# Attention and MoE on one core: weight conversion moved to the start, out of two PSUM banks, and the first batch in two halves

## Chip, cores and metric

The kernel runs on one NeuronCore of a Trainium2 chip. The metric is the time of one execution on the device, in microseconds. Five engines have queues of their own: PE (TensorE), DVE (VectorE), ACT (ScalarE), POOL (GpSimd) and SP, which here only starts DMAs.

## What is computed

Top-32 attention over 8 batches of 8 heads, 576 tokens and 64 columns a head, and behind it one MoE layer with a squared ReLU over all 4608 tokens. The weights come in 64-bit floats, everything else in 32-bit.

```python
scores = scale * np.matmul(q, k.transpose(0, 1, 3, 2))
kth = np.partition(scores, -top_k, axis=-1)[..., -top_k:-top_k + 1]
scores = np.where(scores >= kth, scores, -1000000000.0)
attn = np.exp(scores - np.max(scores, axis=-1, keepdims=True))
attn = attn / (np.sum(attn, axis=-1, keepdims=True) + 1e-09)
x = np.matmul(attn, v)          # tokens x 512, all heads of a token side by side
r = np.maximum(x @ w_in, 0.0)   # w_in 512 x 2048
out = (s * (r * r) + b) @ w_out # w_out 2048 x 512
```

## The kernel before

**Attention.** Two heads make a pair, four pairs a batch. A pair has nine tiles of 128 query rows (tile 4 mixes the last 64 rows of both heads), so a batch has 36 tiles and the kernel 288. Each tile goes through scores on PE (L363), a copy to SBUF on ACT (L369), the top-32 threshold on DVE (eight L375, then L382 to L391), a check on ACT and POOL (L409, L415), exp on ACT (L423), the mask on DVE (L433), transposes on PE (L462, L463) and the product with V. Where a product has to be exact, each operand is split into a high and a low part; batch 0 ("whole", WHOLE = 1) does without the split of the probabilities. A batch is one piece per pair (FULL), but the last batch is cut in HALVES: the first five tiles of all four pairs, then the last four of each.

**MoE.** Blocks of 256 tokens (18), each of 16 chunks of 128 hidden columns, so 288 chunks. A chunk is 12 matmuls into the one buffer `h` (L604), ReLU and square on ACT (L610, L613), a split on POOL (L617, L621) and 6 matmuls into the two buffers `ops` (L627). A block starts when the attention rows of its 256 tokens have been stored for all four pairs.

**Weights.** `w_in` and `w_out` are 64 pieces of 128 x 256. A piece is loaded (L300) into one of four `x` buffers, made 32-bit by three bit operations on DVE (L306, L309, L312; the intermediate `tmp` lies in SBUF, tag `rt`), checked for far exponents (ACT L319, L323, and a PE matmul L326 that accumulates all 64 pieces in the `h` buffer), and split (ACT L329, POOL L332). The column sums of `w_out` for the bias are PE matmuls (L315) that accumulate in both `ops` buffers. So `h` and `ops`, the MoE's PSUM banks, are taken until the last of the 64 pieces is done.

**Order.** Nothing is in loops on the chip. A planner (`Graph.order`) lays the operations of all engines out by a list schedule: of those that could start next on an engine, within SLACK ns of the first, the one with the lowest key. Keys are tile numbers (a chunk's is TURN0 + chunk / TURNS, a weight piece's WTURN * n / 64) plus an offset by kind from PARTS, where each kind also has the planner's slot and duration in ns. LOCK names kinds of which the planner lets DVE and POOL run only one at a time. Each engine then runs its list strictly in that order.

## Time and profile before

| | |
|---|---|
| time, median of 3 runs | 1673.21 us (1672.47 to 1674.39) |
| the profiled execution | 1674.74 us |
| its span, first to last instruction | 1673.0 us |
| mean granted TensorE clock | 0.960 |
| busy: PE, DVE, ACT, POOL | 1486.4, 1393.2, 1251.0, 1292.3 us |

"Busy" is the union of an engine's instructions in time; matmuls are pipelined, so the mean duration of one is longer than the distance between two. The span falls into stages with different work, so the shares over the whole span say little; the section of rows cuts it into six stretches, and counts in them how many tiles and chunks were done.

### The profile page before, as it was taken

To read this page: it belongs to the slowest core of one execution; us is meant where nothing else is said; L and a number is where in the kernel's file an instruction comes from. 1 tells how busy PE (TensorE), PEld (TensorE's weight loads), DVE (VectorE), ACT (ScalarE), POOL (GpSimd) and SP (SyncE) were. 2 spreads that over 40 slices of the span, in tenths; PEclk is the share of its full clock that TensorE was granted. 3 is DMA by queue.
4 is the path that set the end of the run, shared out by engine and by line. 5 is a ranking of instruction groups with operands and counts; after the bars stand their busy time and mean duration, and the time that the engine had idled before them with its cause. 6 is when DMAs were issued, how large, how long until landed. Compare 5 with 4: busy or idle time off the path is not lost.

```text
span 1673.0 us, 33649 instructions
## 1 busy us (share of the span) xinstructions
PE 1486.4 (89%) x9361; PEld 1285.3 (77%) x9361; DVE 1393.2 (83%) x6055; ACT 1251.0 (75%) x2842; POOL 1292.3 (77%) x2111
## 2 busy tenths in 40 slices
PE   3676776799999998989999999999999999999997
PEld 2444444687888887978888888888888889878886
DVE  5999988899999999989999999998989977797000
ACT  4787877887878887877787888887877877786221
POOL 3666665788889887888888988888878988898432
PEclk9986877799999999999999999999999999999999
DMA  4333323222121222122322222222222233442000
GB/s 134 90 94 117 101 88 100 84 58 76 45 83 50 76 60 70 53 83 59 84 54 77 59 73 59 70 58 77 71 57 68 77 105 90 117 131 72 30 13 15
DMA packets 102115, 124.45 MB, mean 74 GB/s; under 512 B 30240, under 2 KB 65056, under 8 KB 101920
## 3 DMA queue, kind: packets, MB, share of 16 engines
q1 hardware_dynamic: 101920, 122.22, 25.5%
q8 instruction: 77, 1.26, 0.3%
q14 instruction: 118, 0.97, 0.2%
HBM read 60.56 MB, written 21.50 MB: 49 GB/s over the span
## 4 chain that ended last, share of the span: by engine, by line
PE 37%; DVE 33%; ACT 9%; DMA 6%; POOL 5%; issue 5%; SPq 4%; POOLq 0%; ACTq 0%; DVEq 0%
PE h L604 12%; PE ops L627 11%; DVE cand L375 8%; DVE e L433 6%; DVE chk L429 4%; DVE pl L473 4%; PE tp L462 4%; PE s_ps L363 4%; SPq L709 2%; DMA kr<-in_kq_dram 2%; ACT sc L369 2%; ACT sg L409 2%; PE av L493 1%; DVE cand L384 1%; POOL wt L415 1%
## 5 line engine op out<-in xcount | busy, mean ns | idle before, releaser
L415 POOL TENSOR_TENSOR wt<-sc,sg 128x576 f32<-128x576 f32 x288 | 402.6, 1398 | 50.3 <-ACT sg L409 17.5
L604 PE MATMUL h<-x,wih 128*128 128x256 f32 x2176 | 421.6, 288 | 11.4 <-ACT rt L610 8.3
L375 DVE MAX8 cand<-sc 128x8 f32<-128x72 f32 x2304 | 392.2, 219 | 44.5 <-ACT sc L369 43.4
L604 PEld LDWEIGHTS h<-x,wih 128*128 128x128 f32 x2176 | 347.1, 190 | 32.9 <-ACT rt L610 17.5
L604 PE MATMUL h<-x,wil 128*128 128x256 f32 x1088 | 307.6, 283 | 0.0
L433 DVE SCALAR_TENSOR_TENSOR e<-sc,chk,e 128x576 f32<-128x576 f32 x288 | 281.5, 979 | 1.7
L409 ACT ACTIVATE sg<-sc,nb 128x576 bf16<-128x576 int16 x288 | 222.0, 771 | 51.3 <-POOL wt L415 25.4
L462 PE MATMUL tp<-idr,e 128*128 128x128 f32 x1152 | 188.4, 288 | 64.3 <-DVE e L433 35.1
L369 ACT ACTIVATE sc<-s_ps 128x576 f32<-128x576 f32 x288 | 185.7, 645 | 64.5 <-DVE e L433 41.1
L429 DVE MAX8 chk<-wt 128x8 f32<-128x584 f32 x288 | 218.2, 758 | 10.9 <-POOL wt L419 9.7
L423 ACT ACTIVATE e<-sc,nb 128x576 f32<-128x576 f32 x288 | 222.0, 771 | 7.1 <-POOL nb L403 3.8
L621 POOL TENSOR_TENSOR gl<-rt,gh 128x256 fp32r<-128x256 f32 x288 | 217.3, 757 | 12.2 <-PE ops L627 1.3
L462 PEld LDWEIGHTS tp<-idr,e 128*128 128x128 f32 x1152 | 135.0, 146 | 106.0 <-issue 35.0
L604 PEld LDWEIGHTS h<-x,wil 128*128 128x128 f32 x1088 | 207.2, 190 | 0.0
L627 PE MATMUL ops<-woh,gh 128*128 128x512 f32 x576 | 195.2, 406 | 7.2 <-DVE osb L634 4.5
L610 ACT ACTIVATE rt<-h 128x256 f32<-128x256 f32 x288 | 109.1, 379 | 122.7 <-PE h L604 112.9
L473 DVE TENSOR_TENSOR pl<-tp,ph 128x512 fp32r<-128x512 f32 x252 | 172.9, 686 | 30.6 <-ACT ph L468 26.1
L363 PE MATMUL s_ps<-ka,qs 128*128 128x288 f32 x512 | 162.0, 330 | 33.8 <-ACT sc L369 14.8
L627 PE MATMUL ops<-woh,gl 128*128 128x512 f32 x576 | 188.7, 399 | 0.9 <-POOL gl L621 0.8
L627 PE MATMUL ops<-wol,gh 128*128 128x512 f32 x576 | 187.6, 398 | 0.0
L617 POOL TENSOR_SCALAR gh<-rt 128x256 fp32r<-128x256 f32 x288 | 123.2, 430 | 79.1 <-PE ops L627 57.1
L468 ACT ACTIVATE ph<-tp 128x512 fp32r<-128x512 f32 (+1 forms) x288 | 169.5, 589 | 11.7 <-PE tp L462 9.6
(98 smaller groups left out, 3362.9 us busy)
## 6 DMA issues: line engine op xcount, KB each, us to landing
kr<-in_kq_dram SPq DMA_DIRECT2D x72, 288.0 KB, 3.2
ka<-kb SPq DMA_DIRECT2D x72, 144.0 KB, 3.3
kb<-ka SPq DMA_DIRECT2D x72, 144.0 KB, 3.1
out_dram<-osb SPq DMA_DIRECT2D x36, 256.0 KB, 2.0
kr<-in_v_dram SPq DMA_DIRECT2D x56, 160.0 KB, 2.4
x<-in_moe_w_in_dram SPq DMA_DIRECT2D x32, 256.0 KB, 3.1
qs<-ka SPq DMA_DIRECT2D x128, 64.0 KB, 2.0
qs<-kb SPq DMA_DIRECT2D x128, 64.0 KB, 2.0
```

The source lines that it names most:

```text
L363: nc.tensor.matmul(flat[:, cs], st, kx[:, cs], start=(m == 0), stop=(m == last))
L369: nc.scalar.activation(t.sc, t.flat, AF.Identity)
L375: nc.vector.max(t.cand[:, g * 8 : g * 8 + 8], t.sc[:, g * GW : (g + 1) * GW])
L409: nc.scalar.activation(t.sg, t.sc.bitcast(I16)[:, 1::2], AF.Sign, bias=t.half, scale=-1.0, accum_out=t.cnt[:, 0:1])
L415: nc.gpsimd.tensor_tensor(out=t.wt[:, :S], in0=t.sc, in1=t.sg, op=ALU.mult)
L423: nc.scalar.activation(t.e, t.sc, AF.Exp, bias=t.nb, scale=scale)
L429: nc.vector.max(t.pair.chk[:, t.i, 0:PADS], t.wt)
L433: nc.vector.scalar_tensor_tensor(t.e, t.sc, chk[:, PADS - 1 : PADS], t.e, op0=ALU.is_ge, op1=ALU.mult, accum_out=chk[:, PADS : PADS + 1])
L462: nc.tensor.transpose(tp[:, c, :], t.e[:, c * P : (c + 1) * P], idf)
L473: nc.vector.tensor_tensor(out=pl[:, :, dst], in0=t.tp, in1=ph[:, :, dst].bitcast(F32), op=ALU.subtract)
L604: nc.tensor.matmul(k.h, wi[a][:, cc, fs], k.x[cc][:, c, :], start=(cc == 0 and i == 0), stop=(cc == NCC - 1 and i == 2))
L627: nc.tensor.matmul(k.ops[t], g[fc][:, t * P : (t + 1) * P], wo[w][:, fc, :], start=(fc == 0 and i == 0), stop=(fc == NFC - 1 and i == 2),)
```

## The change

Five things are done.

1. Two PSUM banks are no longer used for sums over the weights. The far check (`far1`) squares in place on ACT and lets ACT add up each piece (two halves for a piece of `w_out`) into one of 96 columns of an `osb` buffer; `farmax` reduces these. The column sums are 32 matmuls of 512 columns in one run (`colsum`), with a matrix of ones and the split `w_out`, into the `av` buffer, after the last piece has been split; `b` is multiplied in behind it.
2. The intermediate of the bit operations is an `ops` buffer in PSUM, not an SBUF tile; the second operation writes it again, and the third writes the result to SBUF.
3. The pieces come in another sequence (for each 256 columns of `w_in`, its four pieces, then the four of `w_out` that belong to them), with WTURN 21.3 for 40. Some use the four `x` buffers, the rest three more in the space of `pl`, which the first batch doesn't use; so the first `low` of batch 1 waits for all weight work (`wend`), and the first output matmul of the MoE's block 0 for all bit operations (`wbits`).
4. Batch 0 is cut in HALVES as batch 7 is: its first five tiles of four pairs, then the last four. Batch 0's Q, K and V are loaded twice, and its Q and K split twice.
5. The planner's numbers are new: offsets, durations (those of SP and of the bit operations longer), SLACK for PE and ACT, TURN0 and TURNS, and LOCK without the bit operations.

Of the table of numbers one line stands here.

```diff
-    "wload": ("SP", 100, 3500, -0.43), "bits0": ("DVE", 195, 275, -11.69), "bits1": ("DVE", 330, 412, 6.37), "bits2": ("DVE", 325, 405, -2.64),
+    "wload": ("SP", 460, 3300, -2.22), "bits0": ("DVE", 324, 420, -18.25), "bits1": ("DVE", 330, 425, 4.31), "bits2": ("DVE", 330, 415, -7.95),
...
-LOCK = {"mask", "bits0", "bits1", "bits2", *(x for x, y in PARTS.items() if y[0] == "POOL")}
-SLACK = {"PE": 0, "DVE": 86, "ACT": 0, "POOL": 0, "SP": 0}
-TURN0, TURNS = 49.4, 0.992
-WTURN = 40
+LOCK = {"mask", *(x for x, y in PARTS.items() if y[0] == "POOL")}
+SLACK = {"PE": 40, "DVE": 86, "ACT": 14, "POOL": 0, "SP": 0}
+TURN0, TURNS = 51.4, 1.007
+WTURN = 21.3
 
 LATE = (16,)
-BUFS = dict(ph=1, pl=1, p4=1, avu=2, avl=1, x=4, osb=1, sc=4, wt=1, e=2, kr=1, sg=1, rt=2, gh=2, gl=2, vst=2, ka=2, kb=2, qs=2, s_ps=1, tp=1, tq=1, av=1, h=1, ops=2, cand=2, wl=3, m2=2, cnt=3, nb=2, chk=2, ri=2)
+EARLY = 49
+BUFS = dict(ph=1, pl=1, p4=1, avu=2, avl=1, x=4, wraw=3, osb=1, sc=4, wt=1, e=2, kr=1, sg=1, rt=2, gh=2, gl=2, vst=2, ka=2, kb=2, qs=2, s_ps=1, tp=1, tq=1, av=1, h=1, ops=2, cand=2, wl=3, m2=2, cnt=3, nb=2, chk=2, ri=2)
...
+    ones = const.tile([P, P], F32R, name="ones")
+    nc.scalar.activation(ones, idt, AF.Identity, scale=0.0, bias=1.0)
     bias = const.tile([P, DM], F32, name="bias")
-    brow = [ps_o.tile([P, DM], F32, name="ops", tag="ops", bufs=2) for _ in range(2)]
     mid = const.tile([P, 1], F32, name="mid")
-    wfar = ps_h.tile([P, WCH], F32, name="h", tag="h", bufs=1)
+    nc.gpsimd.memset(mid, -64.0)
...
-    wsteps = [(wi, w_in, cc, f) for cc in range(NCC) for f in range(DFF // WCH)]
-    wsteps += [(wo, w_out, fc, e) for fc in range(NFC) for e in range(DM // WCH)]
+    wsteps = []
+    for f in range(DFF // WCH):
+        wsteps += [(wi, w_in, cc, f) for cc in range(NCC)]
+        wsteps += [(wo, w_out, f * WCH // P + x, e) for x in range(WCH // P) for e in range(DM // WCH)]
+    def early(n):
+        return n < EARLY and n % 7 < 4
...
         def load(w):
-            w.raw = sb.tile([P, 2 * WCH], I32, name="x", tag="x", bufs=BUFS["x"])
+            if w.early:
+                w.raw = sb.tile([P, 2 * WCH], I32, name="x", tag="x", bufs=BUFS["x"])
+            else:
+                c0 = 2 * WCH * (sum(not early(n) for n in range(w.n)) % 3)
+                w.raw = p_buffers(True)[1].rearrange("p a b -> p (a b)").bitcast(I32)[:, c0 : c0 + 2 * WCH]
             w.hw, w.lw = w.raw[:, 1::2], w.raw[:, 0::2]
             nc.sync.dma_start(
                 out=w.raw, in_=w.src.bitcast(I32)[w.a * P : (w.a + 1) * P, 2 * w.c * WCH : 2 * (w.c + 1) * WCH]
             )
 
         def bits0(w):
-            w.tmp = sb.tile([P, WCH], I32, name="rt", tag="rt", bufs=BUFS["rt"])
+            w.tmp = ps_o.tile([P, DM], F32, name="ops", tag="ops", bufs=2).bitcast(I32)[:, :WCH]
             nc.vector.tensor_scalar(w.tmp, w.hw, 5, 2, op0=ALU.logical_shift_left, op1=ALU.logical_shift_right)
 
         def bits1(w):
-            nc.vector.scalar_tensor_tensor(w.lw, w.lw, 29, w.tmp, op0=ALU.logical_shift_right, op1=ALU.bitwise_or)
+            nc.vector.scalar_tensor_tensor(w.tmp, w.lw, 29, w.tmp, op0=ALU.logical_shift_right, op1=ALU.bitwise_or)
 
         def bits2(w):
-            nc.vector.scalar_tensor_tensor(w.lw, w.hw, -(1 << 30), w.lw, op0=ALU.bitwise_and, op1=ALU.bitwise_or)
-        def colsum(w):
-            nc.tensor.matmul(brow[w.c][:, :WCH], bmat, w.lw.bitcast(F32), start=(w.a == 0), stop=(w.a == NFC - 1))
...
         def far1(w):
-            w.ck = sb.tile([P, WCH], F32R, name="gh", tag="gh", bufs=BUFS["gh"])
-            nc.scalar.activation(w.ck, w.hw.bitcast(F32), AF.Square, bias=mid)
-        def far2(w):
-            nc.tensor.matmul(wfar, idr, w.ck, start=(w.n == 0), stop=(w.n == len(wsteps) - 1))
+            if not far:
+                far.append(sb.tile([P, DM], F32, name="osb", tag="osb", bufs=BUFS["osb"]))
+            n = 1 if w.dst is wi else 2
+            for x in range(n):
+                cs = slice(x * WCH // n, (x + 1) * WCH // n)
+                k = (w.a * (DFF // WCH) + w.c) if n == 1 else 32 + (w.a * 2 + w.c) * 2 + x
+                nc.scalar.activation(
+                    w.hw.bitcast(F32)[:, cs], w.hw.bitcast(F32)[:, cs], AF.Square, bias=mid, accum_out=far[0][:, k : k + 1]
+                )
...
+    wcol = [None]
+    def colsum():
+        wcol[0] = ps_a.tile([P, 512], F32, name="av", tag="av", bufs=1)
+        for fc in range(NFC):
+            for x in range(2):
+                nc.tensor.matmul(wcol[0], ones, wo[x][:, fc, :], start=(fc + x == 0), stop=(fc == NFC - 1 and x == 1))
+    def bias_out():
+        nc.scalar.activation(bias, wcol[0], AF.Identity, scale=b_col)
...
-        parts = HALVES if b == B - 1 else (FULL,)
+        parts = HALVES if b in (0, B - 1) else (FULL,)
...
-        if pr.part == 2:
+        if pr.part == 2 and not pr.whole:
...
-    walls, wlast = {}, {}
-    whole_h, whole_o = Buf("h"), [Buf("ops") for _ in range(DM // WCH)]
+    walls, wfar, farb, wbits = {}, [], Buf("osb"), []
     for n in range(len(wsteps)):
         w, key = Weight(n), WTURN * n / len(wsteps)
-        raw, rt, ck = Buf("x"), Buf("rt"), Buf("gh")
-        ld = part("wload", key - 6, w.load, new=[raw])
+        raw, rt = Buf("x" if w.early else "wraw"), Buf("ops")
+        ld = part("wload", key - 6, w.load, new=[raw], stream=raw.tag)
         b0 = part("bits0", key, w.bits0, [ld], [rt], [raw])
         b1 = part("bits1", key, w.bits1, [b0], use=[raw, rt])
-        b2 = part("bits2", key, w.bits2, [b1], use=[raw])
-        if w.dst is wo:
-            wlast["o", w.c] = part(
-                "colsum", key, w.colsum, [b2], [whole_o[w.c]] if w.a == 0 else (), [raw] + [whole_o[w.c]] * (w.a > 0), stream=f"colsum{w.c}"
-            )
+        b2 = part("bits2", key, w.bits2, [b1], use=[raw, rt])
+        wbits.append(b2)
         f0 = part("far0", key, w.far0, [b2], use=[raw])
-        f1 = part("far1", key, w.far1, [f0], [ck], [raw])
-        wlast["h"] = part("far2", key, w.far2, [f1], [whole_h] if n == 0 else (), [ck] + [whole_h] * (n > 0))
+        wfar.append(part("far1" if w.dst is wi else "far2", key, w.far1, [f0], [farb] * (n == 0), [raw] + [farb] * (n > 0)))
         hi = part("whigh", key, w.high, [b2], use=[raw])
         walls[w.dst is wo, w.a, w.c] = part("wlow", key, w.low, [hi], use=[raw])
-    part("farmax", WTURN, lambda: nc.vector.tensor_reduce(cm, wfar, axis=AX.X, op=ALU.max), [wlast["h"]], use=[whole_h])
-    wbias = [part("bias", WTURN, lambda c=c: bias_out(c), [wlast["o", c]], use=[whole_o[c]]) for c in range(DM // WCH)]
+    part("farmax", WTURN, lambda: nc.vector.tensor_reduce(cm, far[0][:, :96], axis=AX.X, op=ALU.max), wfar, use=[farb])
+    wcolb = Buf("av")
+    wbias = part("colsum", WTURN, colsum, [walls[True, fc, c] for fc in range(NFC) for c in range(DM // WCH)], [wcolb])
+    wbias = [part("bias", WTURN, bias_out, [wbias], use=[wcolb])]
+    wend = [*walls.values(), *wfar]
...
-                last = part("low", i, lambda t=t: put_low(t), [hi], use=[tpb])
+                last = part("low", i, lambda t=t: put_low(t), [hi] + wend, use=[tpb])
+                wend.clear()
...
-                        [(g1, g1, g2)[i]] + ([walls[True, fc, c] for c in range(DM // WCH)] if i == 0 else []) + wbias,
+                        [(g1, g1, g2)[i]] + ([walls[True, fc, c] for c in range(DM // WCH)] if i == 0 else []) + (wbits if blk + chunk == 1 and i + t == 0 else []),
```

**Where instructions moved.** DVE at the first tile's top-32 (`wl` and `m` are the threshold's steps, `cand` its candidates; L306 to L312 before and L317 to L323 after are a piece's bit operations). Before:

```order
L312 SCALAR_TENSOR_TENSOR x<-x 128x256 x2
L375 MAX cand<-sc 128x8 x9
L382 MAX wl<-cand 128x8
L375 MAX cand<-sc 128x8
L306 TENSOR_SCALAR rt<-x 128x256
L384 MATCH_REPLACE cand<-wl,cand 128x8x3
L309 SCALAR_TENSOR_TENSOR x<-x,rt 128x256
L387 MAX m_306<-cand 128x8
L312 SCALAR_TENSOR_TENSOR x<-x 128x256
L389 MATCH_REPLACE cand<-m_306,cand 128x8x5
L375 MAX cand<-sc 128x8
L391 MAX wl<-cand 128x8
```

After:

```order
L317 TENSOR_SCALAR ops<-x 128x256
L402 MAX wl<-cand 128x8
L317 TENSOR_SCALAR ops<-pl 128x256
L404 MATCH_REPLACE cand<-wl,cand 128x8x3
L320 SCALAR_TENSOR_TENSOR ops<-x,ops 128x256
L407 MAX m_363<-cand 128x8
L323 SCALAR_TENSOR_TENSOR x<-x,ops 128x256
L317 TENSOR_SCALAR ops<-pl 128x256
L409 MATCH_REPLACE cand<-m_363,cand 128x8x5
L320 SCALAR_TENSOR_TENSOR ops<-pl,ops 128x256
L411 MAX wl<-cand 128x8
L323 SCALAR_TENSOR_TENSOR pl<-pl,ops 128x256
```

Ahead of the first `wl` row stand 8 finished pieces before and 17 after, and between the steps of the tile a bit operation now stands at nearly every place. Ahead of the 22nd mask 23 pieces are finished before and 53 after; the 64th is finished ahead of the 50th mask before and of the 29th after.

PE, around attention's product with V in batch 0 (`av`): what stands beside it (`h`, `ops` are the MoE's buffers; `x`, `wih`, `wil` its operands; `gh`, `bmat` belong to the weights). Before:

```order
L493 MATMUL av<-ph,vst 64x256 x4
L494 MATMUL av<-p_431,vst 64x256
L326 MATMUL h<-gh,idr 128x256
L315 MATMUL ops<-x,bmat 128x256 x2
L462 MATMUL tp<-idr,e 128x128 x4
L463 MATMUL tq<-idr,e 64x128
```

After:

```order
L383 MATMUL s_ps<-ka,qs 128x288
L383 MATMUL s_ps<-kb,qs 128x288
L513 MATMUL av<-ph,vst 64x320 x4
L514 MATMUL av<-p_137,vst 64x320
L623 MATMUL h<-x,wih 128x256 x2
L623 MATMUL h<-x,wil 128x256
```

Before, the weights' matmuls write `h` and `ops` there; after, the first chunk of the MoE writes `h`. That is its first row on PE, ahead of the 21st tile's transposes; before, the first chunk stands ahead of the 51st's. Ahead of the 48th tile's transposes stand 14 chunks after and none before.

PE between two tiles of batch 2, some 75 tiles in. Before:

```order
L499 MATMUL av<-p_2746,vst 128x256
L604 MATMUL h<-x,wih 128x256 x2
L604 MATMUL h<-x,wil 128x256
L627 MATMUL ops<-woh,gh 128x512 x2
L627 MATMUL ops<-wol,gh 128x512 x2
L627 MATMUL ops<-woh,gl 128x512 x2
```

After:

```order
L519 MATMUL av<-p_3087,vst 128x256
L482 MATMUL tp<-idr,e 128x128 x4
L483 MATMUL tq<-idr,e 64x128
L564 MATMUL s_ps<-idr,avl 128x128 x4
L567 MATMUL s_ps<-idr,ri 128x128
```

After, no chunk stands there: two blocks (32 chunks) of batch 0's tokens are done, and the third needs tokens of batch 1, whose last tile is the 72nd. Ahead of the 81st tile's transposes stand 31 chunks before and 35 after, ahead of the 288th's 247 in both.

## Rows read from the trace of the kernel before

**Rows 1.** Windows, six stretches: length, busy us (instructions), granted clock, DMA share, GB/s

```profile
0.00:140.00 140.00, 86.22 (x353) 56.30 (x353) 111.75 (x527) 99.03 (x219) 82.37 (x143) 0.91 0.39 109
140.00:305.00 165.00, 115.01 (x456) 77.23 (x457) 148.35 (x624) 123.31 (x284) 104.09 (x158) 0.76 0.32 96
305.00:471.00 166.00, 151.78 (x998) 134.75 (x998) 155.11 (x664) 135.18 (x309) 138.75 (x225) 0.97 0.24 67
471.00:1333.00 862.00, 813.90 (x5474) 731.12 (x5473) 796.18 (x3498) 697.78 (x1583) 735.72 (x1202) 0.99 0.24 68
1333.00:1537.50 204.50, 195.36 (x1304) 174.33 (x1303) 173.87 (x732) 158.13 (x357) 176.46 (x290) 1.00 0.36 105
1537.50:1673.00 135.50, 124.14 (x786) 111.56 (x784) 7.98 (x18) 37.56 (x95) 54.87 (x96) 0.98 0.06 19
```

**Rows 2.** The same, mask L433 alone; each tile has two records

```profile
0.00:140.00 140.00, 19.81 (x44) 0.91 0.39 109
140.00:305.00 165.00, 25.14 (x52) 0.76 0.32 96
305.00:471.00 166.00, 33.10 (x66) 0.97 0.24 67
471.00:1333.00 862.00, 167.22 (x341) 0.99 0.24 68
```

**Rows 3.** The same, hidden matmuls L604 alone, PE and PEld; 12 a chunk

```profile
305.00:471.00 166.00, 53.13 (x366) 47.46 (x366) 0.97 0.24 67
471.00:1333.00 862.00, 297.59 (x2050) 268.52 (x2049) 0.99 0.24 68
1333.00:1537.50 204.50, 77.57 (x542) 71.75 (x542) 1.00 0.36 105
1537.50:1673.00 135.50, 67.42 (x504) 65.63 (x503) 0.98 0.06 19
```

**Rows 4.** Windows, a stretch of the tail, all instructions

```profile
1550.00:1600.00 50.00, 49.70 (x317) 44.84 (x316) 1.50 (x2) 15.10 (x39) 23.04 (x40) 1.00 0.07 22
```

**Rows 5.** Lines: busy us, mean ns | idle before; the bit operations on DVE

```profile
L309 DVE SCALAR_TENSOR_TENSOR x<-x,rt 128x256 int32<-128x256 int32 x64 | 30.8, 483 | 0.1
L312 DVE SCALAR_TENSOR_TENSOR x<-x 128x256 int32<-128x256 int32 x64 | 28.7, 450 | 0.1
L306 DVE TENSOR_SCALAR rt<-x 128x256 int32<-128x256 int32 x64 | 23.8, 372 | 18.5 <-DMA x<-in_moe_w_in_dram 15.7 <-DMA x<-in_moe_w_out_dram 2.4
```

**Rows 6.** By source line, first two bit operations: duration min/median/max ns, first and last start

```profile
L306 DVE TENSOR_SCALAR rt<-x x64: 268/283/1495, 6.6 to 305.9; 128x256 int32<-128x256 int32 x64
...
L309 DVE SCALAR_TENSOR_TENSOR x<-x,rt x64: 376/416/1361, 7.5 to 314.3; 128x256 int32<-128x256 int32 x64
```

**Rows 7.** Lines: the weights' ACT and POOL work

```profile
L323 ACT ACTIVATE gh<-x,mid 128x256 fp32r<-128x256 f32 x64 | 32.8, 515 | 0.0
L319 ACT ACTIVATE x<-x 128x256 f32<-128x256 int32 x64 | 27.4, 433 | 21.0 <-DVE x L312 20.9
L332 POOL TENSOR_TENSOR wol<-x,woh 128x256 fp32r<-128x256 f32 x32 | 26.4, 829 | 25.7 <-ACT woh L329 25.5
L329 ACT ACTIVATE wih<-x 128x256 fp32r<-128x256 f32 x32 | 13.4, 423 | 0.0
```

**Rows 8.** Windows, third bit operation L312 alone; one a piece

```profile
0.00:140.00 140.00, 9.52 (x23) 0.91 0.39 109
140.00:305.00 165.00, 17.48 (x38) 0.76 0.32 96
```

**Rows 9.** Lines: an accumulator's read on ACT; a 256-column DVE operation with a PSUM input

```profile
L409 ACT ACTIVATION_READ_ACCUMULATOR sg<-sc,nb 128x1 f32 x288 | 54.9, 191 | 0.0
...
L555 DVE TENSOR_TENSOR avu<-avu,s_ps 128x256 f32<-128x256 f32 x64 | 24.1, 412 | 6.4 <-PE s_ps L545 4.9 <-PE s_ps L548 1.3
```

**Rows 10.** Lines: the low part of K and Q on POOL

```profile
L699 POOL TENSOR_TENSOR kb<-kr,ka 128x576 fp32r<-128x576 f32 x72 | 106.2, 1476 | 30.6 <-ACT ka L695 26.8 <-DVE cand L375 2.7
```

**Rows 11.** Lines: MoE output matmuls of 512 columns; the weights' far matmul

```profile
L627 PE MATMUL ops<-woh,gh 128*128 128x512 f32 x576 | 195.2, 406 | 7.2 <-DVE osb L634 4.5 <-POOL gh L617 2.6
L326 PE MATMUL h<-gh,idr 128*128 128x256 f32 x64 | 28.1, 440 | 34.8 <-ACT gh L323 34.7
```

More of the change, by code (lines that the diff above doesn't have):

```diff
@@ new lines @@
+    "half": ("POOL", 147, 190, -0.83), "max": ("POOL", 125, 190, -4.75), "side": ("ACT", 759, 860, 0.36), "win": ("POOL", 1250, 1290, 2.95),
+    "exp": ("ACT", 666, 767, 7.55), "wmax": ("DVE", 668, 754, 1.25), "pad": ("POOL", 270, 310, -5.26), "mask": ("DVE", 742, 825, -1.42),
+    "put": ("PE", 502, 690, -5.99), "high": ("ACT", 478, 595, 5.13), "low": ("DVE", 590, 675, 2.59),
+    "resth": ("ACT", 290, 392, 4.04), "restl": ("DVE", 520, 560, 9.55), "av": ("PE", 147, 330, -3.61), "avout": ("ACT", 320, 400, -3.74),
@@ L806, in rows @@
             lo = part("kqlow", key, lambda j=j: kq_low(pr, j), [hi], [kb], [raw, ka])
[L807 removed]
+            qp = part("qplace", key, lambda j=j: q_place(pr, j), [lo], [qs], [ka, kb], n=2 * sum(c in pr.tiles for c in (0, 2)))
             ps = [qp]
```

52 lines of the change are left out of this document (21 added, 31 removed).

## Prediction

> **What bounds the kernel now.** I began with the busy time by stretch [rows 1] and then counted, in the same stretches, the tiles by their masks [rows 2] and the chunks by their hidden matmuls [rows 3]. Six stages come out. Up to 140 us 22 tiles are done and no chunk; from 140 to 305 us 26 tiles, still no chunk; from 305 to 471 us 33 tiles and 30.5 chunks (366 / 12); from 471 to 1333 us 170.5 tiles and 170.8 chunks; up to 1537.5 us 37 tiles and 45.2 chunks; and behind it a tail of 42 chunks without attention, 135.5 us.
>
> In the first two stages DVE is the busiest engine (111.8 of 140 and 148.4 of 165 us, 80% and 90%), PE has a third of its time free, and its granted clock is down to 0.76 in the second, between its levels of 1.2 and 2.4 GHz. These stages are dear: 6.4 us a tile (305 / 48) against 5.06 later (862 / 170.5), because all the weight work lies in them, and the MoE can't fill PE since its banks are held until the last piece.
>
> From 305 us on PE and DVE are both nearly full (94% and 92% in the long stage). Which of them sets the pace is told by the next stage, where a tile has more chunks beside it: 37 tiles at 5.06 us would be 187 us, it took 204.5, and it did 8.1 chunks more than tiles. So a chunk more cost 17.4 / 8.1 = 2.15 us, while DVE fell to 85%. In the tail, with PE alone at 99%, 50 us hold 317 matmuls, 17.6 chunks of 18, 2.84 us each [rows 4]. So PE bounds there, and a chunk taken out of the mixed stages is worth 2.15 to 2.84 us, as long as DVE isn't reached: it works 796.2 / 170.5 = 4.67 us a tile.
>
> **The change, stage by stage.** The order of the changed kernel gives what lies in each stage; I keep the stages by tile (22, 48, 81, 288).
>
> *Weights earlier.* Of the 64 pieces, 53 instead of 23 are converted ahead of the 22nd mask; the trace has the same 23, and 38 in the second stage [rows 8]. A piece costs DVE 372 + 483 + 450 = 1.305 us [rows 5], ACT 433 + 515 + 423 = 1.37 us and POOL some 0.82 us [rows 7].
>
> *The bit operations in PSUM.* Their price is unknown. The nearest row is a 256-column DVE operation with one input in PSUM, 412 ns [rows 9]; three of these make 1.24 us. In SBUF the medians are 283 and 416 ns for the first two, and some take over 1.3 us [rows 6], which makes the means so long. So a piece may cost anything from 1.1 (the SBUF medians, with 417 for the third) to 1.35 us; I leave 1.305, nearest to what was measured on these very operations. The ends are -13 and +3 us over 64 pieces.
>
> The first operation, with one input, is much faster at its median (283 ns) than the PSUM row (412 ns) [rows 6, 9]. The Trainium skill, "VectorE: DVE Perf Modes", section "Why PSUM operands drop a tier", says that a PSUM operand rules out the mode that takes two 32-bit elements at a time. By that rule the first operation would lose its short time and a piece would cost the 1.24 us; without it 283 + 412 + 412 = 1.11 us, 8 us less over 64 pieces.
>
> *To tile 22 (140 us before).* DVE 111.8 + 30 x 1.305 = 151 us. ACT 99.0 + 30 x 1.37 = 140 us, and the far check now reads ACT's accumulator, some 78 times by then (once for a piece of w_in, twice for one of w_out) at up to 191 ns [rows 9], so 140 to 155 us. Two engines tie. 28 us of DVE's idle time here can take some of it. At DVE's 90% of the second stage it is 168 us, +28; at its own 80% 189 us, with all idle time filled 155 us. I take 168, the row of the stage in which work lay ready.
>
> *To tile 48 (165 us before).* 27 pieces fewer, -35 us on DVE: 113 us; four more half pairs add 16 small DVE operations, each below 412 ns, 3 us of at most 6.6: 116 us. PE loses the far matmuls (440 ns each [rows 11]) and the column sums in between, and gets 14 chunks, 14 x 2.84 = 40 us of its 50 idle ones; its clock should rise with that. At 91% for DVE 128 us, -37. Bounds 122 (95%) and 136 (85%). Both stages together: 296 for 305 us, -9, between 277 and 325.
>
> *Loading batch 0 twice.* Eight more K and Q splits cost POOL 8 x 1476 ns = 12 us [rows 10], ACT and SP less. POOL has 57 and 61 us free in the first two stages [rows 1], so I cost them at nothing; with POOL full it would be 12 us.
>
> *The run of column sums.* 32 matmuls in a row, at 406 ns a 512-column matmul [rows 11] at most 13 us; they wait for POOL's last piece, and behind them on PE stand the transposes and scores of the next tiles. ACT, DVE and the mask wait for those, but four score buffers hold up to four tiles, 19 us of DVE's work. 0 to 13 us; I take +2, since the cover is longer than the run.
>
> *Tiles 48 to 81 (166 us before).* 21 chunks for 30.5. On PE this is worth 9.5 x 2.15 = 20 us or more, but DVE is next: 155.1 us less three pieces, 151 us. At its own 93% 162 us, at 100% 151. I take 158, -8. PE stands without chunks for some tiles after the 72nd (block 3 needs batch 1), and its clock may fall there.
>
> *Tiles 81 to 288 (1066.5 us before).* 35 chunks are done instead of 31 at the start, 247 in both at the end: 212.25 instead of 216 to do, -3.75 x 2.15 = -8 us (2.84 makes -11; with DVE as the bound 0).
>
> *Tail.* The same 41 chunks: 0. The waits of `low` and of the first output matmul for the weights lie behind the 29th mask in the order, before the 37th tile and the second chunk need them: 0.
>
> Sum: -9 + 2 - 8 - 8 = -23. The profiled span is 1673.0 us, the execution's own time 1674.74, the median 1673.21; span and median agree, so I subtract from the median: **1650 us**.
>
> **Rivals.**
>
> *The start stalls (slower).* With ACT, DVE and POOL loaded together, the seven piece buffers are held by whichever is last, attention waits for scores behind bit operations on DVE's strict list, and the first stage keeps its own 80%: 151 / 0.80 = 189 us, +49. The second gains 37 as above, so +12, and the attention is later by that. If the later stages give only 4 (162 for 166 us) and the run of sums costs 2, it ends at 1673 + 12 - 4 + 2 = 1683. It decides from 14 us lost in the first two stages (319 us), which is what I expect back later. For it speaks that DVE and ACT tie, against it that the idle 28 us lie exactly there.
>
> *DVE bounds behind tile 48.* Then fewer chunks are worth nothing to tile 288: 1673 - 9 + 2 - 4 = 1662. For it speaks DVE's 92%, against it the 2.15 us for each chunk more.
>
> *The weights fit into the idle start.* 155 + 122 = 277 us (-28), 155 us for tiles 48 to 81 (-11), -11 behind it: 1623. For it speaks the free PE and the 28 us.
>
> *The lead is lost.* The chunks are early in the order, but their inputs aren't: in-order PE waits for them, tile 48 comes at 305 us and only the 4 us of DVE's next stage are left, 1671 with the sums.
>
> **How the numbers follow.** Forecast (1638 to 1660) 0.44; DVE bounds 0.20; idle start filled 0.12; lead lost 0.08; start stalls 0.16. About 0.2% (3.3 us) is what a measurement of this kernel can tell from no change; within it lies the lost lead. So faster 0.75, same 0.08, slower 0.17. Forecast, DVE bound and lost lead hold 0.72, from 1638 to 1676; the slow start comes in up to 1684 and the filled start from 1626 on, which leaves out the ends of both, under 0.2.
>
> **What would show it.** In windows of the changed kernel: the 22nd mask near 168 us, the 48th near 298 us with some 14 chunks of hidden matmuls, the 81st near 456 us with 35, the last near 1514 us, and a tail of 135 us. A DVE share under 85% to tile 22 would mean the stalled start. 5.0 us a tile in the long stage, or less, means that PE was the bound; an unchanged 5.06 that the lead was worth nothing. The three bit operations should add up to 1.1 to 1.35 us. The forecast is wrong if tile 48 comes after 319 us, or if the new order, by its offsets alone, changes the shares of the long stage: one point of 862 us is 9 us, more than any term here.

## The result, and the profile after

The changed kernel takes 1657.68 us (1656.83 to 1658.04, 4 runs), the kernel before beside it 1673.80 us (1672.47 to 1674.58): a ratio of 0.9903, 95% interval 0.9888 to 0.9919. Forecast was 1650 us in a range of 1626 to 1684, so 23 us of gain against 16 measured. The profiled span is 1655.9 us (1673.0 before).

The first view is the windows of the changed kernel, cut at the same masks as those before (22nd, 48th, 81st, 252nd, 288th): length, busy us of PE, PEld, DVE, ACT and POOL with their instructions, granted clock, DMA share, GB/s. It answers to [rows 1].

```profile
0.00:180.00 180.00, 89.14 (x322) 54.50 (x322) 149.20 (x612) 144.35 (x416) 106.79 (x181) 0.88 0.53 145
180.00:312.00 132.00, 116.24 (x649) 90.73 (x648) 119.71 (x556) 109.62 (x264) 101.23 (x168) 0.88 0.33 86
312.00:465.50 153.50, 132.34 (x828) 115.62 (x828) 147.20 (x658) 124.72 (x278) 124.94 (x205) 0.91 0.28 76
465.50:1318.00 852.50, 804.80 (x5396) 717.26 (x5395) 807.85 (x3497) 699.15 (x1574) 729.37 (x1192) 1.00 0.25 67
1318.00:1523.50 205.50, 196.53 (x1312) 177.62 (x1312) 173.08 (x733) 158.95 (x359) 177.57 (x293) 0.99 0.37 105
1523.50:1656.00 132.50, 121.25 (x768) 108.97 (x766) 7.56 (x19) 36.27 (x91) 53.24 (x93) 0.98 0.06 19
```

The same windows for the mask alone show that the cuts are right; each tile has two records, so 22, 26 and 33 tiles [rows 2].

```profile
0.00:180.00 180.00, 24.90 (x44) 0.88 0.53 145
180.00:312.00 132.00, 25.50 (x52) 0.88 0.33 86
312.00:465.50 153.50, 32.10 (x66) 0.91 0.28 76
```

And for the hidden matmuls, 12 a chunk [rows 3]: 13 chunks in the second stage, 21 in the third, 167 and 45 behind it.

```profile
180.00:312.00 132.00, 23.56 (x159) 21.20 (x159) 0.88 0.33 86
312.00:465.50 153.50, 39.37 (x252) 34.25 (x252) 0.91 0.28 76
465.50:1318.00 852.50, 295.28 (x2004) 266.74 (x2004) 1.00 0.25 67
1318.00:1523.50 205.50, 80.53 (x541) 73.42 (x542) 0.99 0.37 105
```

By the mask that ends each stage:

| stage | before | forecast | after |
|---|---|---|---|
| to the 22nd mask | 137.4 us (cut at 140 in the forecast) | 168 | 179.6 |
| to the 48th | 167.5 | 128 + 2 | 132.2 |
| to the 81st | 165.9 | 158 | 153.6 |
| to the 288th | 1066.5 | 1058 | 1058.1 |
| tail | 135.7 | as before | 132.4 |

DVE's work in the first stage was sized well (149.2 us; 151 in the forecast), ACT's too (144.4; 140 to 155). What was not is how full DVE is: 83%, not 90%. The second stage took 2 us more than forecast, the third 4 us less, and the tail 3 us less than before.

What DVE waited for in the first stage stands in the lines of the first bit operation to 180 us (busy us, mean ns | idle before and what ended it):

```profile
L317 DVE TENSOR_SCALAR ops<-x 128x256 int32<-128x256 int32 x28 | 11.9, 424 | 13.2 <-DMA x<-in_moe_w_in_dram 9.6 <-DMA x<-in_moe_w_out_dram 3.2
...
L317 DVE TENSOR_SCALAR ops<-pl 128x256 int32<-128x256 int32 x26 | 11.0, 423 | 5.6 <-DMA pl<-in_moe_w_in_dram 5.2
```

Of DVE's 30.8 idle us, 18 ended when the load of a weight piece landed.

By source line, the first to the third bit operation of the pieces in the `x` buffers (duration min/median/max in ns, first and last start) answer to [rows 6]:

```profile
L317 DVE TENSOR_SCALAR ops<-x x28: 402/428/430, 6.1 to 131.6; 128x256 int32<-128x256 int32 x28
...
L320 DVE SCALAR_TENSOR_TENSOR ops<-x,ops x28: 407/420/430, 7.1 to 133.6; 128x256 int32<-128x256 int32 x28
...
L323 DVE SCALAR_TENSOR_TENSOR x<-x,ops x28: 403/414/429, 7.8 to 134.3; 128x256 int32<-128x256 int32 x28
```

A piece costs 427 + 420 + 413 = 1.26 us, and none of the 192 operations (those in the `pl` space included) is over 431 ns. Lines of the whole span (busy us, mean ns | idle before) show the mask, the read of ACT's accumulator and half of the column sums:

```profile
L453 DVE SCALAR_TENSOR_TENSOR e<-sc,chk,e 128x576 f32<-128x576 f32 x288 | 300.9, 1046 | 3.4 <-ACT e L443 1.9
...
L336 ACT ACTIVATION_READ_ACCUMULATOR pl<-pl,mid 128x1 f32 x53 | 10.1, 191 | 0.0
...
L354 PE MATMUL av<-woh,ones 128*128 128x512 f32 x16 | 6.4, 400 | 0.0
```

### The profile page after: what moved, and what is told of

It reads as the page before. It is cut to its first block, busy times and chain, and to the rows that moved or that the text cites. A ratio compares the mean times of both kernels' runs of the same rounds, so it can differ in the third digit from the quotient of the medians.

```text
span 1655.9 us, 33717 instructions
## 1 busy us (share of the span) xinstructions
PE 1460.3 (88%) x9265; PEld 1264.7 (76%) x9265; DVE 1404.6 (85%) x6069; ACT 1273.1 (77%) x2978; POOL 1293.2 (78%) x2127
## 4 chain that ended last, share of the span: by engine, by line
DVE 41%; PE 36%; ACT 7%; POOL 5%; issue 5%; DMA 5%; SPq 1%; POOLq 0%; ACTq 0%; DVEq 0%
PE h L623 12%; PE ops L646 11%; DVE cand L395 9%; DVE e L453 9%; DVE chk L449 6%; DVE pl L493 5%; PE tp L482 4%; PE s_ps L383 3%; DVE p L503 2%; POOL wt L435 2%; ACT sc L389 1%; DVE cand L404 1%; DVE cand L409 1%; DMA pl<-in_moe_w_in_dram 1%; ACT sg L429 1%
## 5 line engine op out<-in xcount | busy, mean ns | idle before, releaser
L435 POOL TENSOR_TENSOR wt<-sc,sg 128x576 f32<-128x576 f32 x288 | 398.8, 1385 | 70.2 <-ACT sg L429 24.3
L623 PE MATMUL h<-x,wih 128*128 128x256 f32 x2176 | 427.0, 290 | 8.9 <-ACT rt L629 5.5
L395 DVE MAX8 cand<-sc 128x8 f32<-128x72 f32 x2304 | 400.0, 220 | 22.3 <-ACT sc L389 21.0
L623 PEld LDWEIGHTS h<-x,wih 128*128 128x128 f32 x2176 | 351.5, 191 | 36.4 <-ACT rt L629 15.3
L453 DVE SCALAR_TENSOR_TENSOR e<-sc,chk,e 128x576 f32<-128x576 f32 x288 | 300.9, 1046 | 3.4 <-ACT e L443 1.9
L636 POOL TENSOR_SCALAR gh<-rt 128x256 fp32r<-128x256 f32 x288 | 126.9, 442 | 85.6 <-PE ops L646 60.4
L646 PE MATMUL ops<-woh,gh 128*128 128x512 f32 x576 | 191.8, 401 | 1.5 <-POOL gh L636 1.3
```

The source lines that it names most:

```text
L395: nc.vector.max(t.cand[:, g * 8 : g * 8 + 8], t.sc[:, g * GW : (g + 1) * GW])
L435: nc.gpsimd.tensor_tensor(out=t.wt[:, :S], in0=t.sc, in1=t.sg, op=ALU.mult)
L453: nc.vector.scalar_tensor_tensor(t.e, t.sc, chk[:, PADS - 1 : PADS], t.e, op0=ALU.is_ge, op1=ALU.mult, accum_out=chk[:, PADS : PADS + 1])
L623: nc.tensor.matmul(k.h, wi[a][:, cc, fs], k.x[cc][:, c, :], start=(cc == 0 and i == 0), stop=(cc == NCC - 1 and i == 2))
L646: nc.tensor.matmul(k.ops[t], g[fc][:, t * P : (t + 1) * P], wo[w][:, fc, :], start=(fc == 0 and i == 0), stop=(fc == NFC - 1 and i == 2),)
```

## Experiments

All are measured against the kernel before on the same chip (1670.7 us in the first set of four, 1671.4 in the second, 1672.3 in the third); the changed kernel's own 0.9903 is the number to hold beside their ratios. Where a stage is named, it is cut at the masks in that run's trace.

### Without the lead

The planner may not place a chunk of block 0 before the 48th mask; `gate` holds that mask.

```diff
+            if i == START - 1:      # START = 48
+                gate.append(mk)
...
-                    "h", key, ..., [lo, walls[False, cc, fc * P // WCH]],
+                    "h", key, ..., [lo, walls[False, cc, fc * P // WCH]] + gate * (blk == 0),
```

> The changed kernel, with one edit: the planner may not place a chunk of the first block before the 48th mask. Weights, banks, halves and the planner's numbers stay. In its order 0.8 chunks stand ahead of the 48th tile's transposes (14 in the changed kernel), 31.8 ahead of the 81st (35), 243 ahead of the 288th (247). Theory of the lead: the changed kernel gains because chunks are moved out of stages in which PE bounds. Then tiles 48 to 81 take 166 us again instead of 153.5, the 3 chunks more up to tile 288 and the longer tail cost some 10 us, and the stage before tile 48 gives back at most 5: about 1675 us, the time of the kernel before. Rival: the gain comes from the planner's new numbers or from the banks and bit operations; then it stays at 1656 to 1660.

Measured: 1669.5 us, ratio 0.9994 (0.9975 to 1.0012): the gain is gone. The trace: 48th mask at 312.4 us, 81st at 472.0 with 31 chunks (465.4 with 35 in the changed kernel), 288th at 1520.8 with 243, and a tail of 145.7 us. By itself this speaks for the lead, but most of the loss stands in the tail, and the next run says why that can't be trusted.

### The same kernel, another order

```diff
-TURN0, TURNS = 51.4, 1.007
+TURN0, TURNS = 51.9, 1.007
```

> The changed kernel with TURN0 51.9 for 51.4, half a tile: the order is the same up to tile 108 and another one behind it (244 chunks ahead of the 288th tile's transposes, 247 in the changed kernel). It shows what another order of the long stage is worth by itself. All theories: 1657.7, within 5 us; if it moves by more than 8, differences of that size between the other runs say nothing.

Measured: 1667.9 us, ratio 0.9979 (0.9960 to 0.9997). Half a tile in one number of the planner cost most of the change's gain. The trace puts it in the tail: tile 288 comes at 1521.7 us, 2 us earlier than in the changed kernel, but with 244 chunks instead of 247, and the tail is 142.8 us. So orders of the long stage differ by 10 us, and runs can be compared only where they have as many chunks at tile 288, or stage by stage ahead of it.

### Lead, no lead and no halves with the same tail

Three kernels with TURN0 50.9, whose orders have 246.5 to 246.8 chunks ahead of the 288th tile. The first is the changed kernel with that number alone.

```diff
-TURN0, TURNS = 51.4, 1.007
+TURN0, TURNS = 50.9, 1.007
```

> The changed kernel with TURN0 50.9 for 51.4: another order behind tile 72, with 36 chunks ahead of the 81st tile's transposes and 246.8 ahead of the 288th (35 and 247.2). It is the base for the next two, which have the same TURN0 and as many chunks at the 288th. ctrl (TURN0 51.9) was 10 us slower than the changed kernel with 244 chunks there; if that count decides, this one is back at 1655 to 1662. If orders differ by chance alone, 1655 to 1670.

> nolead (no chunk ahead of the 48th mask) with TURN0 50.9: 0.8 chunks ahead of the 48th tile's transposes, 32.5 ahead of the 81st, and now 246.5 ahead of the 288th, as in a509. So the tail is the same, and what the lead is worth must show in when tile 288 comes. Theory of the lead: 3.5 chunks and the time lost up to tile 81, 10 to 16 us more than a509. Rival: nolead's 12 us came from its order behind tile 81, as ctrl's 10 did; then within 4 us of a509.

Measured: 1662.9 us for the first, 0.9949 (0.9929 to 0.9969), above the 1655 to 1662 that were expected if the chunks at tile 288 decide, so orders with that count alike differ too; 1668.1 us without the lead, 0.9972 (0.9959 to 0.9985). The lead is worth 5 us, not 10 to 16; the two intervals overlap a little, and all but one of the ten times keep the order. Windows of the kernel with the lead (columns as above):

```profile
0.00:179.30 179.30, 87.54 (x320) 53.73 (x320) 148.87 (x611) 143.89 (x415) 106.60 (x181) 0.83 0.52 145
179.30:311.20 131.90, 116.55 (x650) 90.91 (x649) 120.23 (x556) 109.72 (x264) 102.40 (x167) 0.88 0.32 86
311.20:466.10 154.90, 133.58 (x838) 116.00 (x837) 146.41 (x651) 124.81 (x278) 125.10 (x205) 0.92 0.28 76
466.10:1525.20 1059.10, 1000.69 (x6689) 894.30 (x6687) 977.66 (x4239) 858.86 (x1930) 910.70 (x1483) 0.99 0.27 74
```

and of the one without it, from the 22nd mask on:

```profile
178.30:312.60 134.30, 95.84 (x416) 68.31 (x414) 117.29 (x541) 100.72 (x236) 85.83 (x141) 0.75 0.32 85
312.60:474.50 161.90, 149.54 (x1019) 134.95 (x1019) 156.47 (x670) 132.45 (x296) 136.71 (x222) 1.00 0.25 68
474.50:1530.50 1056.00, 1002.96 (x6743) 895.57 (x6742) 972.99 (x4238) 861.32 (x1940) 910.27 (x1491) 1.00 0.27 75
```

The third stage takes 154.9 us with 21.5 chunks and 161.9 with 31.3: 7 us for ten chunks, 0.7 us each, with DVE at 95% and 97% of it (the changed kernel and nolead give the same: 153.6 us with 21, 159.6 with 30.2). The long stage is no longer with 214.3 chunks (1056.0 us) than with 211.5 (1059.1). The mean granted clock shows a second effect: in the second stage it is 0.88 with the MoE and 0.75 without, in the third 0.92 against 1.00, between and at the upper of its levels of 1.2 and 2.4 GHz. PE has little to do where the chunks run out: from the 72nd to the 81st mask 2.8 chunks are done with the lead, at a granted clock of 0.71.

The third kernel is the first with batch 0 in one piece.

```diff
-TURN0, TURNS = 51.4, 1.007
+TURN0, TURNS = 50.9, 1.007
...
-    NJOB = (B + 2) * NPAIR
+    NJOB = (B + 1) * NPAIR
...
-        parts = HALVES if b in (0, B - 1) else (FULL,)
+        parts = HALVES if b == B - 1 else (FULL,)
```

> full0 (batch 0 in one piece) with TURN0 50.9: 36 chunks ahead of the 81st tile's transposes and 246.8 ahead of the 288th, as in a509. At the 81st mask full0 was 9 us earlier than the changed kernel with the same chunks, and lost it again behind it with 244 chunks at the 288th tile. With the tail mended it should keep them: 1645 to 1653, 6 to 10 us faster than a509. Rival: halves are worth nothing either way, within 4 us of a509.

Measured: 1642.2 us, ratio 0.9817 (0.9801 to 0.9833). It beats both kernels, the changed one by 0.9% by these ratios, and its twin by 20 us. On PE the last 6639 of 9265 matmuls of the two traces, from behind the 107th tile on, are the same in the same order. Its windows:

```profile
0.00:169.40 169.40, 86.14 (x327) 56.28 (x327) 140.30 (x615) 141.12 (x411) 98.56 (x174) 0.80 0.44 131
169.40:300.40 131.00, 102.51 (x542) 76.22 (x543) 116.89 (x538) 105.59 (x252) 90.23 (x150) 0.88 0.26 75
300.40:457.30 156.90, 142.79 (x947) 126.07 (x946) 148.89 (x655) 129.82 (x290) 131.54 (x216) 0.99 0.26 71
457.30:1511.20 1053.90, 995.39 (x6677) 889.43 (x6676) 972.04 (x4233) 855.65 (x1927) 908.57 (x1481) 1.00 0.26 75
```

It is 9.9 us earlier at the 22nd mask, 10.8 at the 48th and 8.8 at the 81st, although only 8.3 chunks were done at the 48th (14 in its twin); at the 81st it has 36 to 35.5. In the long stage it gains 5 us more. In the profiled runs the twins are 13.7 us apart (1646.3 and 1660.0), and this profiled run is the slowest of its four. The first stage has the same 53 pieces in both, and DVE is equally full (83%); it has 8.6 us more to do with halves. Two things differ. The first are the splits of K and Q; on POOL, for the kernel with halves and the one without:

```profile
0.00:179.30 179.30, 17.84 (x12) 0.83 0.52 145
```

```profile
0.00:169.40 169.40, 9.90 (x7) 0.80 0.44 131
```

12 against 7 by the 22nd mask, 8 us of POOL's time. The second are the 22 masks on DVE, in the same order (busy us, mean ns | idle):

```profile
L453 DVE SCALAR_TENSOR_TENSOR e<-sc,chk,e 128x576 f32<-128x576 f32 x22 | 24.7, 1127 | 1.9 <-ACT e L443 1.9
```

```profile
L453 DVE SCALAR_TENSOR_TENSOR e<-sc,chk,e 128x576 f32<-128x576 f32 x22 | 19.3, 875 | 0.1
```

On average a mask is 250 ns longer in the first, 5.4 us in all, of the 8.6 us that DVE is busy longer; 2.5 of the rest are L538, a small operation behind each finished piece of a pair. In the long stage before, the median mask takes 816 ns and one in ten over 1.6 us, so the mean tells how many are held up: eight of these 22 take over 1 us with halves, two without.

What holds them up can be read from the trace. The two pairs that follow are start and duration in us, in the kernel with halves: a mask that was held up and what POOL did then, and a mask beside a split of K and Q.

```profile
43.06 1.93 DVE L453 SCALAR_TENSOR_TENSOR e<-sc,chk,e 128x576 f32<-128x576 f32 x1
43.10 1.28 POOL L435 TENSOR_TENSOR wt<-sc,sg 128x576 f32<-128x576 f32 x1 [1.53 <-DVE m L407]
...
143.56 0.80 DVE L453 SCALAR_TENSOR_TENSOR e<-sc,chk,e 128x576 f32<-128x576 f32 x1
...
143.89 1.73 POOL L718 TENSOR_TENSOR kb<-kr,ka 128x576 fp32r<-128x576 f32 x1 [0.40 <-ACT ka L714]
```

Of the eight, six run beside L435, POOL's part of the check of another tile, which started at most 0.25 us before or 0.05 us behind the mask, and two beside the split of a weight piece (L344). None is held up by a split of K and Q alone: three more masks run beside one, for 0.19 to 0.47 us, and take 0.80 to 0.82 us. So the longer masks come from when POOL's other work happens to start, that is from the order, and not from the splits. Other orders say the same: with halves, wspread75 and nofar (both below) have means of 960 and 970 ns for these 22 masks, and without halves full0_kq has 1007.

### Batch 0 in one piece, as first tried

The edit of f509 with TURN0 left at 51.4.

> The changed kernel, with batch 0 in one piece per pair instead of two halves, so Q, K and V of batch 0 are loaded once. In its order 8.5 chunks stand ahead of the 48th tile's transposes (14) and 35.5 ahead of the 81st (35). Theory of the lead: tiles 48 to 81 get 27 chunks instead of 21, 6 x 2.15 = 13 us of which the stages before give back up to 6: 1662 to 1671. Rival: what the first batch in halves gains in lead it loses in double loads and splits; then 1654 to 1660.

Measured: 1656.1 us, 0.9909 (0.9879 to 0.9939), the time of the changed kernel, as the rival said: what it had gained by the 81st mask (456.8 for 465.4 us, 35 chunks in both) it lost again with 244 chunks at tile 288 and a tail of 142.4 us. That led to the run above.

### The intermediate back in SBUF

```diff
-            w.tmp = ps_o.tile([P, DM], F32, name="ops", tag="ops", bufs=2).bitcast(I32)[:, :WCH]
+            w.tmp = sb.tile([P, WCH], I32, name="rt", tag="rt", bufs=BUFS["rt"])
...
-        raw, rt = Buf("x" if w.early else "wraw"), Buf("ops")
+        raw, rt = Buf("x" if w.early else "wraw"), Buf("rt")
```

> The changed kernel, with the intermediate of the bit operations in the SBUF buffers rt, as before; every engine's order is the same row for row. Theory of the lead: the bit operations are as dear in either memory (in the changed kernel 427, 420 and 413 ns, 1.26 us a piece; before 1.305 us), so the time stays within 3 us of 1657.7. Rival: PSUM is what makes the crowded first stage bearable, because in SBUF DVE and POOL hold each other up (some operations before took over 1.3 us); then the first stage is some 10 us longer and the time about 1667.

Measured: 1677.0 us, 1.0039 (1.0021 to 1.0057): slower than the kernel before, and 20 us slower than the changed one with every engine's order the same. The rival is right. By source line (min/median/max), the pieces in the `pl` space:

```profile
L317 DVE TENSOR_SCALAR rt<-pl x36: 263/294/1486, 11.5 to 235.4; 128x256 int32<-128x256 int32 x36
...
L320 DVE SCALAR_TENSOR_TENSOR rt<-pl,rt x36: 400/418/1622, 13.5 to 236.6; 128x256 int32<-128x256 int32 x36
...
L323 DVE SCALAR_TENSOR_TENSOR pl<-pl,rt x36: 399/416/1495, 14.1 to 237.0; 128x256 int32<-128x256 int32 x36
```

Medians are near those of the kernel before (294 for 283 ns, 418 for 416) and none is more than 5 ns above that of the changed kernel, but 45 of the 192 operations take over 600 ns, up to 1.6 us; the 192 together take 106.8 us (80.3 in the changed kernel, 83.6 in the kernel before, with 16 over 600 ns). All 45 run beside work of POOL, for 92% of their time on average (27 of them beside splits of weight pieces, 16 beside L435, 13 beside splits of K and Q, some beside two); of the other 147 only half do. The windows show it where the pieces are:

```profile
0.00:192.70 192.70, 93.10 (x319) 55.88 (x319) 165.62 (x611) 145.00 (x415) 114.41 (x181) 0.79 0.49 135
192.70:330.70 138.00, 118.27 (x650) 91.89 (x649) 126.45 (x557) 110.15 (x263) 104.64 (x167) 0.85 0.30 83
```

DVE is busy 165.6 us to the 22nd mask, 16 more than in the changed kernel, and the mask comes 13 us later; the 48th is 19 us later, and hardly anything changes behind that.

Then the same with the planner told of it, so that it sets bit operations and POOL's work apart:

```diff
-LOCK = {"mask", *(x for x, y in PARTS.items() if y[0] == "POOL")}
+LOCK = {"mask", "bits0", "bits1", "bits2", *(x for x, y in PARTS.items() if y[0] == "POOL")}
...
-                        [...] + (wbits if blk + chunk == 1 and i + t == 0 else []),
+                        [...],
```

> The changed kernel with the intermediate in SBUF, as in tmp_sbuf, but now the planner knows of it: the bit operations are in LOCK again, so it sets none of them beside a POOL operation, and the first output matmul no longer waits for all bit operations. In its order 46 pieces stand ahead of the 22nd mask (53), 16.5 chunks ahead of the 48th tile's transposes (14), 37 ahead of the 81st (35). If the 20 us that tmp_sbuf lost are the time in which DVE and POOL block each other, an order that avoids it gets most of them back at the price of idle time on both: 1658 to 1668, with under 10 bit operations over 600 ns (45 in tmp_sbuf, 0 in the changed kernel). Rival: the order can't keep them apart, since POOL is at work two thirds of that time; then 1670 or more.

Measured: 1689.7 us, 1.0106 (1.0078 to 1.0134). The edit also lets the first output matmul go without waiting for the bit operations. The planner can't buy it back, and doesn't even keep them apart: 49 of the 192 operations take over 600 ns, and all take 104.6 us. The ninth mask comes early, at 83.0 us for 99.6 in the changed kernel, but the 22nd at 186.1 for 179.6, with 46 pieces ahead of it for 53; the 48th mask is at 331 us as in the run before, and the tail has 3 chunks more.

### The weights spread

```diff
-WTURN = 21.3
+WTURN = 75
```

> The changed kernel with WTURN 75 instead of 21.3, so that the weight pieces come later: 43 instead of 53 ahead of the 22nd mask, 53 instead of 64 ahead of the 36th. Chunks ahead of the 48th tile's transposes 12 for 14, of the 81st 34 for 35. If the pieces only add their work on DVE, the 22nd mask comes 13 us earlier (167 for 180 us), the 48th at the same time, and the end is 2 to 4 us later for the lead that is lost: 1660. Rival: the crowded first stage wastes time (DVE only 83% busy there), so that spreading gains: 1645 to 1652.

Measured: 1666.6 us, 0.9977 (0.9959 to 0.9995). The 22nd mask comes at 154.9 us, even earlier than expected, the 48th at 310.1 (311.8 in the changed kernel) with 10.8 chunks, the 81st at 463.9 with 33. Up to there it is the trade that was expected; the rest is a tail of 142.4 us, of the kind that ctrl showed.

### The planner's numbers on the kernel before

SLACK, TURN0, TURNS and PARTS are those of the changed kernel, but for bits0 to bits2, colsum, far1, far2, farmax and bias, which keep their numbers; the code is that of the kernel before.

```diff
-SLACK = {"PE": 0, "DVE": 86, "ACT": 0, "POOL": 0, "SP": 0}
-TURN0, TURNS = 49.4, 0.992
+SLACK = {"PE": 40, "DVE": 86, "ACT": 14, "POOL": 0, "SP": 0}
+TURN0, TURNS = 51.4, 1.007
...
-    "group": ("DVE", 134, 218, 18.68),
+    "group": ("DVE", 134, 218, 22.65),
...
```

> The kernel before with the planner's numbers of the changed one (offsets, durations, SLACK, TURN0, TURNS) except those of the weights' operations; banks, SBUF intermediate, FULL batch 0 and WTURN 40 as before. In its order 0.8 chunks stand ahead of the 48th tile's transposes, 32 ahead of the 81st, 247 ahead of the 288th, as before. Theory of the lead and of PSUM: the numbers alone do nothing, 1668 to 1678. Rival: the new numbers order the long stage better; then 1655 to 1665.

Measured: 1669.2 us, 0.9988 (0.9976 to 1.0001). The numbers alone are not the gain at the end. But they shorten tiles 48 to 81, here from 307.8 us on:

```profile
307.80:462.90 155.10, 147.04 (x990) 131.71 (x991) 147.96 (x654) 130.62 (x295) 135.38 (x217) 0.99 0.25 67
```

155.1 us for 165.9 before, with the same number of chunks (30.4 and 30.3) and the old weight work. The 81st mask comes at 462.9 us, 8 us earlier than before; the long stage then takes 3 us more (1069.7). So the third stage became 11 us shorter without fewer chunks in it.

### First K and Q load earlier

The edit of full0, and the first K and Q load behind two weight pieces instead of seven.

```diff
-        ld = part("wload", key - 6, w.load, new=[raw], stream=raw.tag)
+        ld = part("wload", key - 6 + (12 if n > 1 else 0) * (n < 7), w.load, new=[raw], stream=raw.tag)
```

> Batch 0 in one piece, as in full0 (1656.1), and the first K and Q load issued behind two weight pieces instead of seven. If the start is late because the first scores wait for that load (first two masks at 49 us, with DVE idle for a quarter of that time), they come 4 to 8 us earlier and the end by as much: 1648 to 1652. Rival: DVE has pieces to convert meanwhile, and what it gains on tiles it loses on pieces: 1654 to 1658.

Measured: 1658.7 us, 0.9925 (0.9896 to 0.9954); full0 had 0.9909. The second mask comes at 43.4 for 48.4 us, the 22nd at 171.7 for 170.2: what the tiles gain the pieces lose, as the rival said. The run also bears on f509: it has batch 0 in one piece and as many chunks at tile 288 (246.7, with a tail of 134.7 us), but it comes to the 81st mask 3.7 us later and needs 1058.9 us for the long stage, 5 more, and its ratio is that of the changed kernel. As many chunks at tile 288 make orders comparable in the tail, not ahead of it.

### Without the far check

```diff
-        f0 = part("far0", key, w.far0, [b2], use=[raw])
-        wfar.append(part("far1" if w.dst is wi else "far2", ...))
...
-    part("farmax", WTURN, lambda: nc.vector.tensor_reduce(cm, far[0][:, :96], axis=AX.X, op=ALU.max), wfar, use=[farb])
+    part("farmax", WTURN, lambda: nc.vector.memset(cm, 0.0))
```

> The changed kernel without the check for far exponents of the weights (the two ACT operations a piece and the reduction are left out, cm is set to 0); the rest is as it was, but for the order: 38 pieces ahead of the first mask (21), all 64 ahead of the 9th, 16.5 chunks ahead of the 48th tile's transposes (14). It asks which engine bounds the first stages. If ACT does (it is 79% busy to the second mask), tile 48 comes 15 us or more earlier and the end at 1640 to 1648. If DVE and the chain through it do, tile 48 comes under 6 us earlier: 1650 to 1658.

Measured: 1672.1 us, 1.0002 (0.9990 to 1.0014), slower, though ACT is busy 54 us less. Its first stages:

```profile
0.00:185.40 185.40, 88.53 (x354) 58.47 (x354) 155.62 (x648) 102.82 (x221) 117.69 (x196) 0.91 0.52 151
185.40:301.30 115.90, 106.08 (x663) 85.50 (x662) 110.85 (x522) 95.12 (x209) 95.52 (x160) 1.00 0.33 88
```

The 48th mask is 10.5 us earlier (301.3 us) with 16.5 chunks, between the two expectations; the 252nd is at 1319.0 us with 201 chunks, as late as the changed kernel's. All of it is lost in the order behind tile 81 (1070.7 us to the 288th mask), so the end time says nothing on ACT. For the first stages the answer is half: without the check ACT falls to 55% and DVE is still only 84% busy there, so ACT was not what kept DVE from being full. The lines to the 22nd mask show again what did: 19 of DVE's 29.8 idle us there end with the landing of a weight piece. That ACT's work costs some 10 us by tile 48 is this order against the other, not a price by itself.

## Why the prediction was right, and where not

**The sum.** By stage the span moved by +7 (to the 48th mask), -12, -8 and -3 us, where -7, -8, -8 and 0 were forecast. The first has the wrong sign, and what follows shows that the long stage's -8 did not come from its term; the tail's -3 had none (247.2 chunks are done at tile 288 for 246.0 before, so 1.2 fewer are left for it). That 1650 came within 8 us of the measured time is in good part luck.

**Weights earlier: right in work, 12 us short in time.** DVE's 149 us and ACT's 144 us are as summed. The step that failed is the share: I took 90% from the second stage, "the row of the stage in which work lay ready"; it was 83%, near the 80% of the old first stage, which I had kept for the slower rival. That rival came halfway: by the sign that I had named for it, a share under 85%, it came; the first two stages took 311.8 us, 7 more than before, short of the 319 from which it would have decided. What I had wrong is the idle time: I let it take some of the new work, but 14 of its 28 us were waits for the loads of pieces, which [rows 5] showed, and more pieces brought more of these (18 us of 30.8). The share is 83 or 84% with the pieces spread (wspread75), without the check (nofar) and without halves (f509) alike, with 18 or 19 us of such waits in each. Why the loads come late was not tried. The run of column sums was to cost 2 us: PE did nothing else from 226.5 to 234.2 us, and DVE was idle for 5.8 of the 14 us from 226 to 240, where 1.3 would be its share in this stage, so some 4 us is nearer (an estimate from these windows; no run left it out).

**Loading batch 0 twice: the term that was wrong.** I costed it at nothing, with POOL's idle time as cover, and 12 us without the cover. f509 against a509 says 10 us by the 22nd mask, 9 by the 81st, and 14 to 20 us at the end; of these the 9 by the 81st mask stand in the other order too (full0 against the changed kernel), and what comes behind is order. POOL was 60% busy, so the cover was there for POOL's own time. The cost is on DVE, 8.6 us of work, of which 5.4 are masks held up by POOL. But the trace shows them held up by POOL's part of the check (six of eight) and not by the splits, and with other orders halves don't hold them up so often. So these 10 us are in part a coincidence of this order, and what the halves cost in themselves stays open.

**The bit operations in PSUM: a right price, a wrong question.** 1.26 us a piece lies between my ends of 1.1 and 1.35, and the first operation lost its short form, 283 to 427 ns. The rule of the Trainium skill that I weighed ("VectorE: DVE Perf Modes", section "Why PSUM operands drop a tier"), that any PSUM operand rules out the mode with two 32-bit elements at a time, agrees with the trace. But I compared the price with that of the kernel before, where the pieces are spread; packed into 30 tiles, the SBUF form costs 26 us more on DVE (106.8 for 80.3) and 20 at the end, with every engine's order the same, so the long form is the cheap one. The row that told this was there [rows 6]: maxima of 1.4 to 1.5 us, five times the median of the first operation. Another page would have asked the question: the Trainium skill, "SBUF — State Buffer", section "Who interferes with whom", says that a DVE instruction with two SBUF inputs contends with a GpSimd instruction that reads SBUF, that one in a mode that takes both of its ports contends too, and that one with at most one SBUF input outside those modes doesn't. The trace agrees: 45 of 192 operations were held up with all operands in SBUF (13 of the first operation, with one input, and 32 of the other two) and none with one operand in PSUM.

**Tiles 48 to 81: -12 for -8.** The third stage was DVE's as forecast (96% busy, 153.6 us). But it was not the chunks alone: among kernels with the new weight work ten chunks less are worth 6 to 7 us of it, and newnum_before took 11 us off it with no chunk less. The planner's numbers, which I gave no term here, are a rival for the rest.

**A chunk's price: wrong.** I took 2.15 us from a stage with 1.2 chunks a tile, where DVE had fallen to 85%, and used it for stages with one chunk a tile or fewer, where both engines are nearly full. There ten chunks cost 7 us, and three cost nothing that can be told from the order (the long stage with 212 chunks took 1049 us in nolead and 1058 in the changed kernel). The lead of 14 chunks is worth 5 us, and 14 chunks at tile 48 buy no more by the 81st than 8.3 do (35.5 and 36 with and without halves), because the MoE has tokens for 32 chunks only until batch 1 is done. By the sign that I had named, 5.0 us a tile in the long stage (852.5 us for 170.5 tiles), PE would have been its bound. But the long stage's -8, which came out to the microsecond, did not come from the 3.75 chunks: the kernels with the new weight work have 1049 to 1059 us there, those without the lead too (only the one without the far check has 1071), and both with the old weight work 1067 and 1070. What shortens it I did not find, so the sign does not carry.

**The order: the warning was right.** One point of share in the long stage was said to be worth more than any term. By the ratios, half a tile in TURN0 moved the changed kernel by 8 and 13 us (a509, ctrl) and the one without halves by 15 (full0 against f509). Of the 16 us measured some 8 are then this order against that of a509 (0.9903 for 0.9949, with intervals that nearly meet), 4 the lead, and 5 all the rest together (n509), the halves' cost included.
